# Pooled attention and a PReLU feed-forward network: the output tiles of chunks 1 to 8 stored by ACT's DMA queue

## The chip, the cores and the metric

The kernel runs on one core of a Trainium2 chip. The metric is the time of one execution on the device in microseconds; lower is better. The core has five engines that run side by side, each with its own list of instructions worked off in order: PE (matrix products), DVE and ACT (element-wise work), POOL (element-wise work) and SP, which here only begins DMA transfers. ACT can begin transfers too. A wait at the head of an engine's list holds everything behind it on that engine.

## The reference

Attention over 8 batches and 8 heads, with keys and values averaged over groups of 8 positions, and then a feed-forward network with a PReLU. Cut to its core:

```python
k_p = k.reshape(B, H, Sp, 8, D).mean(axis=3)      # 576 -> 72 positions; v_p alike
attn = softmax(q @ k_p.T / sqrt(D))
x = (attn @ v_p).transpose(0, 2, 1, 3).reshape(4608, 512)
h = x @ w_in                                      # 512 -> 2048
g = max(h, 0) + alpha * min(h, 0)
out = g @ w_out                                   # 2048 -> 512, float32
```

## The kernel before

The 4608 tokens go in 9 chunks of 512 tokens (chunk 0 to chunk 8). Every float32 operand is split into a high and a low float16 part, and each product is three matrix products. Chunk 0 has its own start phase (about the first 200 us, in which weights are loaded and converted as well). From chunk 2 on the first layer (FFN-1) is done in Strassen form: per chunk 4 blocks of 7 products, each product twelve matmuls at L964, with combined weights `wt` that SP loads from a DRAM buffer `ws` (L942, 896 KB each, eight per chunk). A result bank `m` of PSUM (two of them) is emptied by DVE (`join`, L977) or ACT (`keep`, L973) into buffers `c`; ACT scales them (L1115), DVE does the PReLU (L1119), ACT makes the high part `g` (L1123), POOL the low one (L1126). The second layer runs one block behind the first, on the rows of `g`: a step is six matmuls at L885 to L887 that add into one of four PSUM tiles of 128 tokens by 512. One product or one such step is called a piece below; PE alternates between them.

While PE works on a chunk, the attention of the next chunk is prepared beside it: loads of k, q and v by SP (L279), the maxima of q, k and v (ACT L407, a small PE product L233 on the tile `pd` that ACT writes at L230), scores (PE L667), softmax (DVE, ACT, POOL), four transposes `aT<-apad` that SP begins (L577), and the mix with v (PE L677).

After its last step an output tile is scaled into SBUF by ACT (`out_tile`, L875) and stored by `store` (L880), 256 KB. The SBUF tile comes from the pool `fp` with three buffers (the kind "f"), which also serves tiles of the attention (`ks`, `vs`); a buffer comes free when the store has landed. The four output tiles of a chunk thus need a buffer that an earlier store gives back.

The order on every engine is not the order of the code. All operations are recorded in a plan (`_Plan.add`: engine, assumed duration, what it comes after, a rank, and the kinds of buffers that it takes and gives). `_Plan.emit` then plays the plan through with the assumed durations and emits the operations in the order that this gives; an operation on "SP" counts as done `DMA_HOP` = 2.0 us after its end, on another engine 0.12 us (`HOP`). Since each choice depends on the times before it, another duration or engine for one operation reorders much of what comes later on all engines.

Of the kernel before, what the change touches and what calls it, by code (L numbers as in the profile page):

```python
# [21 lines left out]
SP = S // POOL  # L22
# [3 lines left out]
P = 128  # L26
# [60 lines left out]
class _Plan:  # L87
# [13 lines left out]
        self.fill = fill  # L101
        self.ops, self.room, self.port = [], {k: n * [0.0] for k, n in room.items()}, 0.0

    def add(self, engine, us, emit, *after, rank=0.0, take=None, give=None, two=False, ahead=0.0):
        kinds = lambda x: (x,) if isinstance(x, str) else tuple(x or ())
        op = dict(engine=engine, us=us, emit=emit, after=after, rank=rank, n=len(self.ops), take=kinds(take),
                  ahead=ahead, give=kinds(give), two=two or engine == "Pool")
        self.ops.append(op)
        return op

    def emit(self):
        ops, free = self.ops, {}
        mine = {id(op) for op in ops}
        follow, left, since, ready = [[] for _ in ops], [], len(ops) * [0.0], {}
        for op in ops:
            after = [d for d in op["after"] if id(d) in mine]
            for d in after:
                follow[d["n"]].append(op)
            left.append(len(after))
            if not after:  # L120
                ready.setdefault(op["engine"], {})[op["n"]] = op
        for _ in ops:
            picks = []
            for engine, some in ready.items():
                at = []
                for n, op in some.items():
                    t = max(free.get(engine, 0.0), since[n], self.port if op["two"] else 0.0)
                    need = {k: op["take"].count(k) for k in op["take"]}
                    if any(len(self.room[k]) < x for k, x in need.items()):
                        continue  # L130
                    t = max([t] + [sorted(self.room[k])[x - 1] for k, x in need.items()])
                    at.append((t, op["rank"], n))
                if at:
                    t0 = min(at)[0] + self.NEAR[engine]
                    picks.append(min((x for x in at if x[0] <= t0), key=lambda x: x[1:]))
            t, _, n = min(picks, key=lambda x: (x[0], x[2]))
            op = ops[n]
            engine = op["engine"]
            if engine == "PE" and self.fill:
                gap = t - free.get("PE", 0.0)  # L140
                if gap > self.IDLE:
                    self.fill(int((gap * 0.89 - (0.6 if free.get("PE") else 2.5)) / 0.109))
            free[engine] = t + op["us"]
            if op["two"]:
                self.port = t + op["us"]
            end = t + op["us"] + (self.DMA_HOP if engine == "SP" else self.HOP)
            for kind in op["take"]:
                self.room[kind].remove(min(self.room[kind]))
            for kind in op["give"]:
                self.room[kind].append(end)  # L150
            for x in follow[n]:
                since[x["n"]] = max(since[x["n"]], end + x["ahead"])
                left[x["n"]] -= 1
                if not left[x["n"]]:
                    ready.setdefault(x["engine"], {})[x["n"]] = x
            del ready[engine][n]
            op["emit"]()
# [3 lines left out]
def pooled_attention_prelu_ffn(ctx: ExitStack, tc: tile.TileContext, qT, kT, vT, kN, vN, w1, w2, alpha, out):  # L161
# [5 lines left out]
    nc = tc.nc  # L167
# [707 lines left out]
        nc.scalar.activation(o, ps, AF.Copy, scale=out_scale(c, i))  # L875
        return o

    def store(c, i, o):
        t0 = c * CH + i * P
        return nc.sync.dma_start(out=out[t0:t0 + P, :], in_=o)  # L880

    def ffn2_step(c, i, f, ps, first, final):
        ts_ = slice(i * P, i * P + P)
# [189 lines left out]
    def steady(plan, xd, td, used, loaded, made):  # L1073
        FFN, HIGH = 1e6, -1e6
# [74 lines left out]
        def out_items(c, b):  # L1149
            for k in range(2):  # L1150
                for i in range(TPC):
                    def item(k=k, i=i):
                        first, final = b == k == 0, b == NB - 1 and k == 1
                        fs = (4 * b + k, 4 * b + 2 + k)

                        def products():
                            if first:
                                acc[c, i] = ps_h.tile([P, DM], F32, tag="h", name="o")
                            for f in fs:
                                ffn2_step(c, i, f, acc[c, i], first and f == fs[0], final and f == fs[1])  # L1160
                        x = pe(1.3, products, *(g_at[c, b][f] for f in fs), take="h" if first else None,
                               give="g" if k == 1 and i == TPC - 1 else None)
                        if final:
                            o = []
                            y = plan.add("ACT", 0.69, lambda: o.append(out_tile(c, i, acc.pop((c, i)))), x, scaled["o", c],
                                         rank=HIGH, take="f", give="h")
                            plan.add("SP", 0.8, lambda: store(c, i, o[0]), y, rank=HIGH, give="f")
                    yield item

        for n in range(NB * (NC - 1) + 1):  # L1170
            c, b = 1 + n // NB, n % NB
# [61 lines left out]
```

## Time and profile before

| | us |
|---|---|
| median of 3 runs (lowest, highest) | 855.45 (854.04, 858.91) |
| the profiled execution | 858.35 |
| its span, from the first to the last instruction | 856.6 |
| PE busy | 807.3 |
| DVE busy | 591.7 |
| ACT busy | 478.7 |
| POOL busy | 426.0 |

The span is what the trace covers; the rest of the execution's time lies around it. PE's busy time counts matmuls as overlapping, so it is read here only for where PE is not busy. The clock that the throttle granted to PE and the DMA traffic are given by the profile as well.

### The profile page before, as it was taken

Reading aid. Unit: us, or ns where it says so; the run is one execution under the profiler, and the core shown is the slowest. Engines: PE = TensorE matmul, PEld = TensorE weight load, DVE = VectorE, ACT = ScalarE, POOL = GpSimd, SP = SyncE. Lnnn points to the kernel's source line nnn. Section 1 sums busy time; section 2 is a strip of 40 time slices with the busy share of each in tenths; the row PEclk is TensorE's granted clock in tenths of the full one; section 3 lists DMA queues with packets and bytes.
Section 4 is the critical chain, followed back from the end, with each engine's and each line's share of the span. In section 5 each row is a group of like instructions: output and inputs, shape, how many; then the busy total and the mean of one; then the engine's idle time right before and its main releaser. Section 6 shows DMA issues by size and latency. Waiting matters only on the chain.

```text
span 856.6 us, 15008 instructions
## 1 busy us (share of the span) xinstructions
PE 807.3 (94%) x5971; PEld 497.1 (58%) x5971; DVE 591.7 (69%) x880; ACT 478.7 (56%) x858; POOL 426.0 (50%) x433
## 2 busy tenths in 40 slices
PE   5679987899999889999999999999999999999998
PEld 4444453344456556665666666666666666666664
DVE  4969879897798776766986786677757544433442
ACT  6779996475455455655656564654655444223223
POOL 0255646767865466347546844653444434222222
PEclk9899999999999999999999999999999999999999
DMA  9678337229724891693298159525645534223201
GB/s 330 230 168 316 128 78 176 83 96 256 236 93 154 239 253 69 155 281 106 103 267 255 52 154 247 146 94 160 183 125 142 145 109 169 87 88 135 86 1 50
DMA packets 106198, 133.69 MB, mean 156 GB/s; under 512 B 78320, under 2 KB 80944, under 8 KB 106128
## 3 DMA queue, kind: packets, MB, share of 16 engines
q1 hardware_dynamic: 106128, 132.74, 51.5%
q8 instruction: 47, 0.77, 0.4%
q14 instruction: 23, 0.19, 0.1%
HBM read 96.48 MB, written 16.78 MB: 132 GB/s over the span
## 4 chain that ended last, share of the span: by engine, by line
PE 61%; DVE 9%; DMA 6%; ACT 4%; issue 2%; POOL 1%; SPq 0%; DVEq 0%; ACTq 0%; POOLq 0%
PE m L964 24%; PE o L885 10%; PE o L886 10%; PE o L887 10%; DMA qraw<-qT_dram 3%; DVE c L1119 2%; PE x L677 2%; PE s L667 1%; DVE c L977 1%; PE h L840 1%; PE h L842 1%; PE h L841 1%; ACT c L1115 1%; DMA aT<-apad 1%; DMA vraw<-vT_dram 1%
## 5 line engine op out<-in xcount | busy, mean ns | idle before, releaser
L964 PEld LDWEIGHTS <-wt 128*128 128x128 f16 x2352 | 228.3, 98 | 72.1 <-issue 3.3
L977 DVE TENSOR_TENSOR c<-m,c 128x512 f32<-128x512 f32 x196 | 134.6, 688 | 163.6 <-PE m L964 158.5
L1126 POOL TENSOR_TENSOR g<-c,g 128x512 f16<-128x512 f32 x112 | 136.4, 1229 | 205.4 <-ACT g L1123 130.6
L886 PE MATMUL o<-w,g 128*128 128x512 f16 x544 | 206.8, 380 | 4.6 <-DVE w L762 4.6
L885 PE MATMUL o<-w,g 128*128 128x512 f16 x544 | 207.3, 381 | 0.3 <-POOL g L1126 0.3
L887 PE MATMUL o<-w,g 128*128 128x512 f16 x544 | 206.8, 380 | 0.0
L964 PE MATMUL m<-x,wt 128*128 128x256 f16 x1344 | 166.1, 273 | 4.2 <-DVE c L977 2.3
L1115 ACT ACTIVATE c<-c,rp 128x512 f32<-128x512 f32 x112 | 75.5, 714 | 118.9 <-DVE c L977 114.6
L1119 DVE SCALAR_TENSOR_TENSOR c<-c,al 128x512 f32<-128x512 f32 x112 | 102.7, 939 | 31.0 <-ACT c L1115 30.5
L964 PE MATMUL m<-xt,wt 128*128 128x256 f16 x1008 | 123.8, 273 | 0.0
L887 PEld LDWEIGHTS <-g 128*128 128x128 f16 x576 | 56.6, 98 | 73.7 <-issue 6.6
L885 PEld LDWEIGHTS <-g 128*128 128x128 f16 x576 | 56.5, 98 | 52.5 <-issue 4.3
L1123 ACT CAST g<-c 128x512 f16<-128x512 f32 x112 | 67.9, 617 | 32.0 <-DVE c L1119 31.0
L886 PEld LDWEIGHTS <-g 128*128 128x128 f16 x576 | 56.6, 98 | 46.2 <-issue 1.1
L489 POOL TENSOR_TENSOR vraw<-vraw 72x512 f32<-72x512 f32 (+1 forms) x56 | 63.4, 1145 | 30.7 <-DMA vraw<-vT_dram 17.7
L569 POOL TENSOR_TENSOR apad<-e,apad 128x448 f16<-128x448 f32 x36 | 38.4, 1067 | 59.5 <-ACT apad L566 58.8
L566 ACT CAST apad<-e 128x576 f16<-128x576 f32 x72 | 46.1, 669 | 23.0 <-POOL e L561 11.0
L859 POOL TENSOR_TENSOR g<-t,g 128x512 f16<-128x512 f32 x32 | 39.3, 1240 | 35.7 <-ACT g L856 28.1
L627 POOL TENSOR_TENSOR xf<-xf 128x256 f32<-128x256 f32 x48 | 38.0, 791 | 35.1 <-ACT xf L622 32.3
L841 PE MATMUL h<-x,w 128*128 128x512 f16 x128 | 48.5, 379 | 1.5 <-DVE x L604 1.5
L840 PE MATMUL h<-x,w 128*128 128x512 f16 x128 | 48.6, 380 | 0.0
L842 PE MATMUL h<-x,w 128*128 128x512 f16 x128 | 48.5, 379 | 0.0
(156 smaller groups left out, 1081.1 us busy)
## 6 DMA issues: line engine op xcount, KB each, us to landing
wt<-ws SPq DMA_DIRECT2D x56, 896.0 KB
w<-w_dram SPq DMA_DIRECT2D x16, 1024.0 KB
out_dram<-o SPq DMA_DIRECT2D x36, 256.0 KB
qraw<-qT_dram SPq DMA_DIRECT2D x17, 512.0 KB
vraw<-vT_dram SPq DMA_DIRECT2D x28, 288.0 KB
kraw<-kT_dram SPq DMA_DIRECT2D x12, 576.0 KB
ws<-o SPq DMA_DIRECT2D x8, 512.0 KB
ws<-w SPq DMA_DIRECT2D x8, 256.0 KB
```

The costliest lines, as they stand in the source:

```text
L489: nc.gpsimd.tensor_tensor(out=o, in0=y, in1=z, op=ALU.add)
L840: nc.tensor.matmul(ps, w[:, 1, ks_], x[:, 0], start=(n == 0), stop=False)
L841: nc.tensor.matmul(ps, w[:, 0, ks_], x[:, 1], start=False, stop=False)
L885: nc.tensor.matmul(ps, g[:, 1, ts_], w[:, 0], start=first, stop=False)
L886: nc.tensor.matmul(ps, g[:, 0, ts_], w[:, 1], start=False, stop=False)
L887: nc.tensor.matmul(ps, g[:, 0, ts_], w[:, 0], start=False, stop=final)
L964: nc.tensor.matmul(ps[:, p], w[:, lw], x[:, lx], start=(j == n == 0), stop=(j == 1 and n == 2))
L977: nc.vector.tensor_tensor(out=self.part(b, o), in0=self.t[b, m], in1=self.part(b, i), op=ALU.add)
L1115: nc.scalar.activation(u, u, AF.Copy, scale=rp[:, f:f + 1])
L1119: nc.vector.scalar_tensor_tensor(out=u, in0=u, scalar=al[:, f:f + 1], in1=u, op0=ALU.mult, op1=ALU.max)
L1123: nc.scalar.copy(out=g_tile(c, f)[:, 0], in_=st.row(b, i, p)[0])
L1126: nc.gpsimd.tensor_tensor(out=g_tile(c, f)[:, 1], in0=st.row(b, i, p)[0], in1=g_tile(c, f)[:, 0], op=ALU.subtract)
```

## The change

Each of the 32 output tiles of chunks 1 to 8 is stored by a transfer that ACT begins (`nc.scalar`), directly from ACT's list; the four of chunk 0 stay on SP. In the plan the store is an operation of ACT of 0.1 us where it was one of SP of 0.8 us; the flag `far` keeps its 2.0 us until it counts as done.

```diff
--- before.py
+++ after.py
@@ -101,10 +101,10 @@
         self.fill = fill
         self.ops, self.room, self.port = [], {k: n * [0.0] for k, n in room.items()}, 0.0
 
-    def add(self, engine, us, emit, *after, rank=0.0, take=None, give=None, two=False, ahead=0.0):
+    def add(self, engine, us, emit, *after, rank=0.0, take=None, give=None, two=False, ahead=0.0, far=False):
         kinds = lambda x: (x,) if isinstance(x, str) else tuple(x or ())
         op = dict(engine=engine, us=us, emit=emit, after=after, rank=rank, n=len(self.ops), take=kinds(take),
-                  ahead=ahead, give=kinds(give), two=two or engine == "Pool")
+                  ahead=ahead, give=kinds(give), far=far or engine == "SP", two=two or engine == "Pool")
         self.ops.append(op)
         return op
 
@@ -143,7 +143,7 @@
             free[engine] = t + op["us"]
             if op["two"]:
                 self.port = t + op["us"]
-            end = t + op["us"] + (self.DMA_HOP if engine == "SP" else self.HOP)
+            end = t + op["us"] + (self.DMA_HOP if op["far"] else self.HOP)
             for kind in op["take"]:
                 self.room[kind].remove(min(self.room[kind]))
             for kind in op["give"]:
@@ -875,9 +875,9 @@
         nc.scalar.activation(o, ps, AF.Copy, scale=out_scale(c, i))
         return o
 
-    def store(c, i, o):
+    def store(c, i, o, by=nc.sync):
         t0 = c * CH + i * P
-        return nc.sync.dma_start(out=out[t0:t0 + P, :], in_=o)
+        return by.dma_start(out=out[t0:t0 + P, :], in_=o)
 
     def ffn2_step(c, i, f, ps, first, final):
         ts_ = slice(i * P, i * P + P)
@@ -1164,7 +1164,7 @@
                             o = []
                             y = plan.add("ACT", 0.69, lambda: o.append(out_tile(c, i, acc.pop((c, i)))), x, scaled["o", c],
                                          rank=HIGH, take="f", give="h")
-                            plan.add("SP", 0.8, lambda: store(c, i, o[0]), y, rank=HIGH, give="f")
+                            plan.add("ACT", 0.1, lambda: store(c, i, o[0], nc.scalar), y, rank=HIGH, give="f", far=True)
                     yield item
 
         for n in range(NB * (NC - 1) + 1):
```

Up to the stores of chunk 1 all engines have the same rows in the same order; behind them the plan's order differs on all of them. On SP, at the stores of chunk 1 (`wt<-ws_125` and so on are the loads of combined weights, `ws_130<-w` and `ws_128<-o` writes of such weights to DRAM):

```order
 L922 DMA ws_128<-o_2611 128x2048
 L942 DMA wt<-ws_125 128x3584
-L880 DMA out_dram<-o 128x512 x2
-L942 DMA wt<-ws_126 128x3584
-L880 DMA out_dram<-o 128x512 x2
+L942 DMA wt<-ws_126 128x3584
 L942 DMA wt<-ws_127 128x3584
 L904 DMA ws_130<-w_275 128x1024
 L905 DMA ws_130<-w_275 128x2x256
```

The two loads of weights that stood behind two and four stores now follow the load of `ws_125` directly.

On ACT, at the same place (`o` is the output tile, `c` the buffers of FFN-1, `g` the high part): before,

```order
L875 ACTIVATE o<-o,os 128x512
L1115 ACTIVATE c<-c,rp 128x512 x2
L875 ACTIVATE o<-o,os 128x512
L1123 CAST g<-c 128x512 x2
L875 ACTIVATE o<-o,os 128x512
L1115 ACTIVATE c<-c,rp 128x512
L875 ACTIVATE o<-o,os 128x512
L1115 ACTIVATE c<-c,rp 128x512
```

and now

```order
L875 ACTIVATE o<-o,os 128x512
L880 DMA out_dram<-o 128x512
L1115 ACTIVATE c<-c,rp 128x512 x2
L875 ACTIVATE o<-o,os 128x512
L880 DMA out_dram<-o 128x512
L1123 CAST g<-c 128x512 x2
L875 ACTIVATE o<-o,os 128x512
L880 DMA out_dram<-o 128x512
L1115 ACTIVATE c<-c,rp 128x512
L875 ACTIVATE o<-o,os 128x512
L880 DMA out_dram<-o 128x512
L1115 ACTIVATE c<-c,rp 128x512
```

Each store follows the activation that writes its tile and waits for it; the scaling and casts of FFN-1 stand behind it. Most of these stores also wait, by the program, for one transfer of SP that was begun earlier and shares the store's semaphore.

On SP, at the stores of chunk 2, in the time in which the attention of chunk 4 is transposed and the k, q and v of chunk 5 are loaded: before,

```order
L577 DMA_TRANSPOSE aT<-apad_95 128x16x128
L279 DMA kraw<-kT_dram 128x1152
L880 DMA out_dram<-o 128x512
L577 DMA_TRANSPOSE aT<-apad_96 128x16x128
L880 DMA out_dram<-o 128x512
L942 DMA wt<-ws_127 128x3584
L880 DMA out_dram<-o 128x512
L942 DMA wt<-ws_128 128x3584
L880 DMA out_dram<-o 128x512
L279 DMA kraw<-kT_dram 128x1152
L279 DMA qraw<-qT_dram 128x1024
```

and now

```order
L577 DMA_TRANSPOSE aT<-apad_95 128x16x128
L279 DMA kraw<-kT_dram 128x1152
L577 DMA_TRANSPOSE aT<-apad_96 128x16x128
L279 DMA kraw<-kT_dram 128x1152
L942 DMA wt<-ws_127 128x3584
L577 DMA_TRANSPOSE aT<-apad_95 128x16x128
L942 DMA wt<-ws_128 128x3584
L279 DMA qraw<-qT_dram 128x1024
```

The four stores are gone from between the loads, and the third transpose stands ahead of the load of q, where it stood behind it.

On PE the pieces keep their order, and only the attention's products move between them. The mix of chunk 3 stands 3 pieces earlier than before, that of chunk 4 stands 7 pieces earlier, those of chunks 5 and 6 stand 8 and 4 pieces later, and those of chunks 7 and 8 stand where they were. The three small products L233 on the maxima of chunk 5 (k and q) stood ahead of the mix of chunk 4 and now stand behind it, 7 pieces later than before; those of chunk 7 stand one piece later. On SP, two transposes and two loads of weights stood between the loads of k for chunk 7 and that of its q; now none does.

## Rows read from the trace of the kernel before

**Rows 1.** The page: the span, and the busy time of each engine.

```profile
span 856.6 us, 15008 instructions
PE 807.3 (94%) x5971; PEld 497.1 (58%) x5971; DVE 591.7 (69%) x880; ACT 478.7 (56%) x858; POOL 426.0 (50%) x433
```

**Rows 2.** Busy time by stretches of 50 us from 250 us on: stretch, its length, busy us (instructions) of PE, PE's weight loads, DVE, ACT and POOL, the granted clock, the DMA share and GB/s.

```profile
250.00:300.00 50.00, 46.16 (x394) 30.12 (x393) 42.04 (x60) 26.20 (x54) 29.22 (x29) 1.00 0.58 170
300.00:350.00 50.00, 46.44 (x362) 29.93 (x360) 34.84 (x55) 28.13 (x56) 29.52 (x34) 0.97 0.55 159
350.00:400.00 50.00, 48.01 (x386) 31.81 (x385) 32.27 (x55) 26.06 (x43) 26.39 (x27) 1.00 0.79 207
400.00:450.00 50.00, 50.00 (x440) 32.47 (x437) 43.48 (x65) 30.34 (x59) 27.97 (x29) 1.00 0.52 163
450.00:500.00 50.00, 48.61 (x391) 32.43 (x389) 34.63 (x51) 29.28 (x58) 34.31 (x35) 1.00 0.50 156
500.00:550.00 50.00, 47.80 (x374) 31.16 (x372) 34.86 (x55) 26.56 (x44) 25.39 (x24) 1.00 0.78 207
550.00:600.00 50.00, 50.00 (x448) 32.71 (x447) 38.38 (x58) 28.65 (x57) 27.45 (x30) 1.00 0.35 111
```

**Rows 3.** What PE waited for between 250 and 600 us: total us, times, longest.

```profile
PE pm L233 <- ACT pd L230: 3.6, 2, 2.0
PE x L677 <- DMA aT<-apad: 2.9, 1, 2.9
PE m L964 <- DVE c L977: 2.3, 2, 2.0
PE m L964 <- DMA wt<-ws: 1.5, 2, 1.3
PE s L667 <- ACT e L546: 1.3, 2, 0.7
PE x L677 <- ACT xf L622: 0.7, 1, 0.7
```

**Rows 4.** What SP's queue waited for at the line of the stores, in the whole run: total us, times, longest.

```profile
SPq L880 <- ACT o L875: 160.5, 32, 48.4
```

**Rows 5.** SP's instructions in order of time around the stores of chunk 1 and up to the last transpose of chunk 3: start, us (two or more in a row are merged with their waits), line.

```profile
264.94 2.94 SPq L880 DMA_DIRECT2D out_dram<-o  x2
267.93 0.42 SPq L942 DMA_DIRECT2D wt<-ws  x1
270.14 1.63 SPq L880 DMA_DIRECT2D out_dram<-o  x2
271.86 0.39 SPq L942 DMA_DIRECT2D wt<-ws  x1
...
276.09 0.32 SPq L922 DMA_DIRECT2D ws<-o  x1
...
310.63 5.93 SPq L577 DMA_TRANSPOSE aT<-apad  x1
```

**Rows 6.** PE and DVE in order of time in the same stretch: start, us, instruction; in brackets the idle time before it and what ended it.

```profile
272.63 0.83 PE L964 MATMUL m<-x,wt 128*128 128x256 f16 x6 [1.35 <-DMA wt<-ws]
283.20 1.48 PE L964 MATMUL m<-x,wt 128*128 128x256 f16 x12 [2.03 <-DVE c L977]
...
285.82 1.47 PE L964 MATMUL m<-x,wt 128*128 128x256 f16 x12
...
282.45 0.69 DVE L977 TENSOR_TENSOR c<-m,c 128x512 f32<-128x512 f32 x1 [2.53 <-DMA ws<-o]
```

**Rows 7.** PE in order of time at the mix of chunk 3.

```profile
318.61 0.91 PE L677 MATMUL x<-aT,v 88*64 88x320 f16 x12 [2.95 <-DMA aT<-apad]
319.45 2.13 PE L964 MATMUL m<-x,wt 128*128 128x256 f16 x12
```

**Rows 8.** SP's instructions in order of time around the stores of chunk 2.

```profile
358.64 3.35 SPq L577 DMA_TRANSPOSE aT<-apad  x1
362.09 0.52 SPq L880 DMA_DIRECT2D out_dram<-o  x1
...
369.09 0.33 SPq L880 DMA_DIRECT2D out_dram<-o  x1
...
370.25 0.39 SPq L279 DMA_DIRECT2D qraw<-qT_dram  x1
...
385.65 5.06 SPq L577 DMA_TRANSPOSE aT<-apad  x1
```

**Rows 9.** PE in order of time: the small products on the maxima and the mix of chunk 4, and the small product on the maxima of chunk 7.

```profile
390.11 0.22 PE L233 MATMUL pm<-pd,ones 128*128 128x128 bf16 x1 [1.99 <-ACT pd L230]
...
395.52 1.08 PE L677 MATMUL x<-aT,v 88*64 88x256 f16 x16
...
542.31 0.22 PE L233 MATMUL pm<-pd,ones 128*128 128x128 bf16 x1 [1.56 <-ACT pd L230]
```

**Rows 10.** ACT in order of time: the fourth output tile of chunk 2, and what it waited for.

```profile
368.37 0.69 ACT L875 ACTIVATE o<-o,os 128x512 f32<-128x512 f32 x1 [1.25 <-DMA out_dram<-o]
```

**Rows 11.** The views of two lines, the stores and the transposes: how many, the shortest, median and longest time in ns that SP was held by one, first and last start, forms.

```profile
L880 SPq DMA_DIRECT2D out_dram<-o x36: 332/338/530, 172.3 to 853.6; - x36
...
L577 SPq DMA_TRANSPOSE aT<-apad x36: 1694/2652/5930, 40.6 to 683.5; - x36
```

**Rows 12.** The chain that ended last, its last piece: start, us, engine, tile and line.

```profile
852.90 0.69 ACT o L875
```

## The prediction

> **What bounds the kernel now.** I read the page first: PE is busy in 807.3 of 856.6 us, no other engine above 591.7 [rows 1]. So I looked for the places where PE is not busy, by stretches. The change can act only from the first store of chunk 1 on, at 264.94 us [rows 5], since all engines have the same list up to there. From 250 to 600 us PE is busy for 337.0 of 350 us: the seven stretches leave 3.84, 3.56, 1.99, 0, 1.39, 2.20 and 0 us, together 12.98 us [rows 2]. The rows to see there are the full ones: where PE shows 50.00 of 50 it sets the pace alone, and no better list for SP can win anything. So nearly all that can be won is 13 us of waits, plus what a slow clock costs after one of them. The third view tells what these waits were for [rows 3]: small products on maxima that ACT brings late (3.6 us), the mix of chunk 3, which waits for a transpose (2.9), banks of FFN-1 that DVE empties late (2.3), loads of combined weights (1.5), and smaller ones behind ACT.
>
> Are the stores behind these? In the whole run SP's list stands at them for 160.5 us until ACT has the tile ready [rows 4]. That alone costs nothing; what matters is which load stands behind one and is waited for.
>
> **The change part by part.** The sum is made on the profiled execution, 858.35 us. The median of the runs, 855.45, is 2.9 us lower, and I take these 2.9 off at the end.
>
> A. Stores of chunk 1. SP was at the stores from 264.94 to 267.88, and only then began the load of the weights that PE waited 1.35 us for at 272.63; the next load came after two more stores, at 271.86 [rows 5, 6]. In the new list both follow the earlier load directly and wait only for PE to release their buffers, by the order some pieces before the end of the first output tile. They can start some 3 to 6 us earlier, and the wait of 1.35 us goes. The second wait has a longer path: DVE finishes a tile of combined weights, SP writes it out from 276.09, and the buffer comes free only when it has landed, which held DVE's join until 282.45 and PE until 283.20 [rows 5, 6]. The write took 6.3 us, with the late loads ahead of it. With those out of the way I expect about the 4.7 us that the load begun at 267.93 took to PE's start at 272.63, or less. But ACT now begins four stores before its cast of that tile, at 0.34 us each [rows 11], and DVE gets it a little later. Between 3.38 us (both waits gone) and 0 I take 2.5 won: the first wait shifts PE, but the second is set by DVE, so the two do not add up.
>
> B. Mix of chunk 3. PE waited 2.95 us for the fourth transpose, and the product behind it then took 2.13 us where the same twelve matmuls took 1.48 [rows 6, 7]; the granted clock of this stretch of 50 us was 0.97, that is 1.5 us lost [rows 2]. So up to 4.5 us hang on this wait. In the new list the loads of v ahead of that transpose no longer stand behind a write of weights, so it comes earlier than 310.63 [rows 5]. But PE meets the mix 3 pieces earlier, and with A's 2.5 us that is about 6.4 us (a piece takes 1.3 us: a product begun at 283.20 and the next at 285.82 have a step between them [rows 6]). What the transpose wins is needed in full. I put nothing down here; the ends are 4.5 won and 2 lost.
>
> C. Stores of chunk 2. The first store is followed by a transpose that holds SP for 3.35 us, so that the second store leaves only at 362.09; the fourth tile on ACT waits 1.25 us for a buffer; its store leaves at 369.09; and the load of q for chunk 5 behind it at 370.25 [rows 8, 10]. Its maxima reach PE late: 1.99 us of wait at 390.11 [rows 9]. Without stores between them these loads can leave earlier, and the small products moved 7 pieces back. The wait should go. But the load of q now stands behind the third transpose, which waits for POOL and ACT, and the mix of chunk 4 comes first. Between 1.99 and 0 I take the middle, 1.0.
>
> D. Maxima of chunk 7: 1.56 us of wait at 542.31 [rows 9]. The load of their q no longer stands behind two transposes. Middle again: 0.8.
>
> E. Cost on ACT. The trace shows no store begun by ACT. On SP one holds the list for 0.332 to 0.530 us, median 0.338 [rows 11]: 32 of them are 10.8 us on ACT, which is busy for 478.7 of 856.6 [rows 1], so most of it falls into gaps. 16 of them (chunks 1 to 4) lie in the stretch with waits, 5.4 us. PE waits for ACT at five places there (rows of `pd`, `e` and `xf`) [rows 3]. If half of these have a store shortly ahead, that is 0.8 us; the ends are 0 and 5.4. From 550 us on PE is full [rows 2] and the cost is hidden behind it as long as ACT has its gaps.
>
> F. The end. The last output tile is scaled at 852.90 for 0.69 us, and the span ends 3.0 us later, with its store [rows 1, 12]. ACT needs 0.69 plus 0.34 us for a tile, less than the 1.3 us in which PE delivers one, so nothing queues there: 0.
>
> Sum: 858.35 - 2.5 - 1.0 - 0.8 + 0.8 = 854.85; less 2.9 gives **852.0 us**.
>
> **The rivals.** 1. The waits go for good: A 3.4, B 4.5 (without the wait the clock stays up), C 2.0, D 1.6, against 0.8 on ACT, 10.7 us in all; I take 9, since a new order hardly leaves none: 846.5 us. For it: every one of these waits has a load behind a store or a transpose in its history. Against it: the mix of chunk 3 comes up earlier too.
>
> 2. No change, 855.5 us. PE is full in two of seven stretches [rows 2], and what is won early is given back at the next product of the attention, which the plan has moved forward in proportion. SP has time: what is truly saved is 32 times 0.338 us of its list [rows 11], on which PE does not wait. The Trainium skill (DMA: Bandwidth & Descriptors, Issuing engines are not separate DMA queues) says as much of transfers begun on several engines: they run on the same DMA engines, and only the time of beginning one is saved. The rows speak against that being all, since SP's list stood 160.5 us at these stores [rows 4].
>
> 3. Slower: the mix of chunk 4 comes before its inputs. PE meets it 7 pieces earlier, 9.1 us. Before, its fourth transpose left SP at 385.65 and the mix ran at 395.52 without a wait [rows 8, 9]. If that transpose leaves no earlier, PE is 9.1 us behind at this point, less C's 2.0: 855.45 + 7.1 = 862.5 us. It decides when the transpose leaves less than about 5 us earlier. For it: the load of q and the transposes share SP, and ACT now has stores between its casts. Against it: SP lost 362.09 to 369.09 to stores there [rows 8].
>
> 4. ACT is held while SP begins a transpose. SP is held for 1.7 to 5.9 us by one, 36 times 2.65 us or 11% of the span [rows 11]. If a store on ACT had to wait for that, 3 to 4 of 32 would be hit, more in chunks 1 to 4, by 1.3 to 5.9 us each; with half of it on PE's path some 6 us: 858 to 861 us. No row bears on it. The Trainium skill (Perfetto Trace Analysis, DMA Instruction — HWDGE (DVE, Sync)) lets a sequencer wait for a descriptor generator that two sequencers share, which would be this mechanism; no run so far shows it.
>
> **How the numbers follow.** Forecast 0.40, rival 1 0.27, rival 2 0.12, rival 3 0.14, rival 4 0.07. 0.5% of the time, about what a measurement of this kernel can tell from no change, is 4.3 us: faster is below 851.2, slower above 859.7. Faster: rival 1 and an eighth of the forecast, 0.32. Slower: rival 3, most of rival 4: 0.20. The rest is 0.48. The range leaves out the lower edge of rival 1 and most of rival 3: 845.5 to 861 us.
>
> **What would show it.** Right: no wait of PE for `wt` near 270 us, the join near 282 us released 2 us earlier, the load of q for chunk 5 not behind a store, and less than 10 us of idle PE from 250 to 600. Wrong: PE idle for 4 us or more at the mix of chunk 3 or 4 (rival 3), a store on ACT that holds it for over 1 us while SP is at a transpose (rival 4), or new waits behind ACT between 600 and 850, where PE was full.

## The result, and the profile after

The kernel after takes 866.27 us (863.32 to 867.37) where the kernel before took 855.25 us on the same chip: a ratio of 1.0109, 95% interval 1.0081 to 1.0137. It is slower by 11 us, where 3 were to be won, and lies outside the range. Its profiled execution took 865.44 us, so that run and the profiled one of before are 7.1 us apart; the rest is the scatter of single runs. One of the seven runs of old_order_no_hold below took 1404 us; its ratio leaves that run out, and without it the median is 852.20.

The page and the seven stretches of 50 us, against [rows 1] and [rows 2]; q10 is the new queue, ACT's own, with 32 stores:

```profile
span 863.7 us, 15011 instructions
PE 813.2 (94%) x5971; PEld 499.0 (58%) x5971; DVE 589.2 (68%) x880; ACT 478.7 (55%) x858; POOL 423.4 (49%) x433
...
q10 hardware_dynamic: 4608, 8.39, 2.6%
```

```profile
250.00:300.00 50.00, 44.05 (x378) 28.67 (x377) 41.58 (x60) 25.90 (x53) 28.70 (x29) 1.00 0.55 161
300.00:350.00 50.00, 49.75 (x413) 32.42 (x412) 42.43 (x63) 29.70 (x57) 34.32 (x36) 1.00 0.51 169
350.00:400.00 50.00, 44.25 (x326) 28.45 (x324) 27.24 (x43) 24.93 (x41) 27.17 (x27) 0.97 0.76 207
400.00:450.00 50.00, 49.45 (x441) 32.75 (x439) 35.99 (x63) 25.55 (x50) 17.95 (x21) 1.00 0.37 125
450.00:500.00 50.00, 49.43 (x370) 32.20 (x369) 38.45 (x49) 29.24 (x48) 34.81 (x35) 1.00 0.68 193
500.00:550.00 50.00, 46.34 (x367) 30.06 (x366) 33.11 (x57) 28.39 (x58) 22.40 (x25) 0.97 0.64 195
550.00:600.00 50.00, 49.31 (x455) 32.45 (x454) 36.94 (x54) 27.71 (x54) 29.64 (x33) 1.00 0.35 105
```

PE now leaves 17.4 us of these 350, where it left 13.0, and two stretches instead of one have a granted clock of 0.97, which is 1.5 us more lost (0.03 of 50). To see where the loss ends, take ACT at the first output tile of chunk 1 and that of chunk 5, in the kernel before:

```profile
264.23 0.69 ACT L875 ACTIVATE o<-o,os 128x512 f32<-128x512 f32 x1 [2.21 <-PE o L887]
...
614.33 0.69 ACT L875 ACTIVATE o<-o,os 128x512 f32<-128x512 f32 x1 [0.70 <-PE o L887]
```

and in the kernel after:

```profile
265.30 0.69 ACT L875 ACTIVATE o<-o,os 128x512 f32<-128x512 f32 x1 [2.21 <-PE o L887]
...
621.40 0.69 ACT L875 ACTIVATE o<-o,os 128x512 f32<-128x512 f32 x1 [0.91 <-PE o L887]
```

This stretch took 350.1 us and now 356.1. From there to the first output tile of chunk 8 both take 234.6 to 234.7 us, and ahead of the stretch both have the same lists. So 6.0 of the 7.1 us lie in chunks 1 to 4, and the 4.4 us of idle PE and the 1.5 of clock make up 5.9 of them. I use this stretch as a measure below. It is taken from one execution of each run: old_order_act_chunks_5_to_8, which leaves the stores of chunks 1 to 4 as they were, gave 347.1, so 3 us of it can be scatter.

What PE waits for there, against [rows 3]:

```profile
PE m L964 <- ACT c L973: 6.6, 4, 2.9
PE m L964 <- DMA wt<-ws: 4.4, 2, 2.8
PE o L885 <- ACT o L875: 3.0, 1, 3.0
...
PE s L667 <- ACT e L546: 0.7, 1, 0.7
PE x L677 <- DMA aT<-apad: 0.6, 1, 0.6
```

The waits of [rows 3] that the change was to remove are mostly gone: 3.6 us for `pd`, 2.0 of the 2.3 for DVE's join and most of the 2.9 for the transpose; the one for weights grew from 1.5 to 4.4. In their place stand 9.6 us on ACT that were not there, its copy of a product (`c`, L973) and its output tile (`o`, L875). ACT is no busier than it was: 478.7 us in both pages. It stands still. What ACT waited for at L875 from 250 us on, before and then after (total us, times, longest):

```profile
ACT o L875 <- DMA out_dram<-o: 2.6, 3, 1.3
```

```profile
ACT o L875 <- DMA out_dram<-o: 21.8, 5, 5.7
```

The output tile needs one of three buffers, and one comes free only when an earlier store has landed. ACT in order of time at chunk 2, in the kernel after:

```profile
358.94 0.68 ACT L875 ACTIVATE o<-o,os 128x512 f32<-128x512 f32 x1
359.65 0.34 ACTq L880 DMA_DIRECT2D out_dram<-o  x1
...
367.33 0.69 ACT L875 ACTIVATE o<-o,os 128x512 f32<-128x512 f32 x1 [5.43 <-DMA out_dram<-o]
368.04 0.35 ACTq L880 DMA_DIRECT2D out_dram<-o  x1
368.44 0.72 ACT L1115 ACTIVATE c<-c,rp 128x512 f32<-128x512 f32 x1 [0.43 <-ACT o L875]
369.07 0.56 ACT L973 COPY c<-m 128x512 f32<-128x512 f32 x1
...
375.99 0.69 ACT L875 ACTIVATE o<-o,os 128x512 f32<-128x512 f32 x1 [5.74 <-DMA out_dram<-o]
```

ACT's list goes in order: behind the tile that stands at 367.33 is the copy at 369.07, and PE waits for both. PE at the same place, and at chunk 4:

```profile
369.68 1.47 PE L964 MATMUL m<-x,wt 128*128 128x256 f16 x12 [1.86 <-ACT c L973]
...
376.73 0.59 PE L885 MATMUL o<-w,g 128*128 128x512 f16 x1 [2.97 <-ACT o L875]
...
547.39 2.72 PE L964 MATMUL m<-x,wt 128*128 128x256 f16 x12 [2.87 <-ACT c L973]
```

The last row shows the second price: after 2.87 us of standing still, twelve matmuls took 2.72 us, where 1.47 is usual. The granted clock of this stretch (547.39 to 550.11 us) is 0.50, the lower of its two levels (1.2 and 2.4 GHz).

The begin itself is not late: each of the 32 stores begins 0.03 us after its tile is done, so the semaphores that the stores share with SP's transfers held none of them. Why the buffer comes back late is in the chain that ended last. Two pieces of it at chunk 2 before, and at the same chunk after (start, us from the store's begin to its landing):

```profile
362.09 2.61 DMA out_dram<-o
...
365.51 2.77 DMA out_dram<-o
```

```profile
359.65 7.59 DMA out_dram<-o
...
368.04 7.92 DMA out_dram<-o
```

The tile at 367.33 starts 0.09 us after the first of these has landed (359.65 and 7.59 are 367.24), the one at 375.99 0.03 us after the second. SP's list around these two stores, in the kernel after:

```profile
359.40 0.33 SPq L942 DMA_DIRECT2D wt<-ws  x1
362.30 4.51 SPq L577 DMA_TRANSPOSE aT<-apad  x1
366.90 0.53 SPq L942 DMA_DIRECT2D wt<-ws  x1
367.52 0.38 SPq L279 DMA_DIRECT2D qraw<-qT_dram  x1
367.96 0.91 SPq L279 DMA_DIRECT2D vraw<-vT_dram  x2
```

Each store has loads of SP begun just ahead of it (896 KB at 359.40 and at 366.90), and a transpose or more loads behind. In SP's own list the store went first and the loads stood behind it, as [rows 8] show. The records of single packets in the trace give the parts. Of the 32 stores, 11 met no packet of SP on the way to their first: their first packet ran 0.84 to 0.88 us after the begin. For the other 21 it was 1.28 to 4.98 us. Three of these stores, three of the run with stores of 8 KB (below), and one of each kind without SP:

```
store (256 KB)  begun   first packet  last packet ended
chunk 1         268.62  after 3.22    after 5.49 us
chunk 2         359.65        4.14          6.91
chunk 2         368.04        4.11          7.43
chunk 5         622.12        0.84          1.68
store (8 KB)
chunk 2         358.55  after 1.98    after 6.19 us
chunk 2         366.11        3.83          6.59
chunk 4         532.74        4.38          8.56
chunk 8         854.78        0.84          1.05
```

### The profile page after: what moved, and what is told of

Same layout as the page of the kernel before. It is cut to its first block, busy times and chain, and to the rows that moved or that the text cites. A ratio compares the mean times of both kernels' runs of the same rounds, so it can differ in the third digit from the quotient of the medians.

```text
span 863.7 us, 15011 instructions
## 1 busy us (share of the span) xinstructions
PE 813.2 (94%) x5971; PEld 499.0 (58%) x5971; DVE 589.2 (68%) x880; ACT 478.7 (55%) x858; POOL 423.4 (49%) x433
## 4 chain that ended last, share of the span: by engine, by line
PE 59%; DVE 7%; DMA 6%; ACT 5%; POOL 4%; issue 2%; SPq 1%; ACTq 0%; DVEq 0%; POOLq 0%
PE m L964 23%; PE o L885 10%; PE o L887 10%; PE o L886 10%; DMA out_dram<-o 4%; PE x L677 1%; DMA qraw<-qT_dram 1%; PE s L667 1%; PE h L840 1%; PE h L841 1%; PE h L842 1%; POOL g L1126 1%; SPq L577 1%; ACT o L875 1%; POOL vraw L489 1%
## 5 line engine op out<-in xcount | busy, mean ns | idle before, releaser
L1119 DVE SCALAR_TENSOR_TENSOR c<-c,al 128x512 f32<-128x512 f32 x112 | 96.5, 881 | 49.9 <-ACT c L1115 49.6
L841 PE MATMUL h<-x,w 128*128 128x512 f16 x128 | 49.2, 384 | 1.5 <-DVE x L604 1.5
L840 PE MATMUL h<-x,w 128*128 128x512 f16 x128 | 49.3, 385 | 0.0
L842 PE MATMUL h<-x,w 128*128 128x512 f16 x128 | 49.0, 383 | 0.0
```

Source lines behind the costliest of these rows:

```text
L840: nc.tensor.matmul(ps, w[:, 1, ks_], x[:, 0], start=(n == 0), stop=False)
L841: nc.tensor.matmul(ps, w[:, 0, ks_], x[:, 1], start=False, stop=False)
L1119: nc.vector.scalar_tensor_tensor(out=u, in0=u, scalar=al[:, f:f + 1], in1=u, op0=ALU.mult, op1=ALU.max)
```

## The experiments

All times are medians; "before" is the kernel before on the same chip. The last two columns come from each run's profiled execution: ACT's waits at the output tile for landed stores from 250 us on, and the stretch from the first output tile of chunk 1 to that of chunk 5.

| run | us | before | ratio (95%) | ACT waits, us | stretch, us |
|---|---|---|---|---|---|
| the kernel after | 866.27 | 855.25 | 1.0109 (1.0081 to 1.0137) | 21.8 | 356.1 |
| new_order_sp | 869.33 | 856.95 | 1.0143 (1.0114 to 1.0172) | 12.0 | 359.3 |
| old_order_act | 861.83 | 856.95 | 1.0065 (1.0040 to 1.0090) | 13.5 | 352.8 |
| new_order_16_columns | 862.77 | 856.95 | 1.0057 (1.0027 to 1.0087) | 19.8 | 354.0 |
| old_order_16_columns | 853.92 | 856.95 | 0.9947 (0.9925 to 0.9968) | 2.3 | 344.7 |
| new_order_no_hold | 852.03 | 856.22 | 0.9942 (0.9912 to 0.9972) | 1.9 | 341.9 |
| old_order_no_hold | 852.54 | 856.22 | 0.9948 (0.9923 to 0.9973) | 1.9 | 343.2 |
| old_order_extra_starts | 856.74 | 856.22 | 0.9995 (0.9968 to 1.0021) | 4.1 | 347.9 |
| new_plan_late_landing | 863.59 | 856.22 | 1.0076 (1.0042 to 1.0110) | 5.6 | 357.0 |
| old_order_act_chunks_1_to_4 | 859.51 | 856.51 | 1.0030 (1.0001 to 1.0058) | 16.5 | 350.9 |
| old_order_act_chunks_5_to_8 | 856.82 | 856.51 | 0.9997 (0.9966 to 1.0029) | 1.2 | 347.1 |
| new_order_four_buffers | 886.25 | 856.51 | 1.0325 (1.0292 to 1.0357) | 0 | 337.0 |
| old_order_four_buffers | 886.04 | 856.51 | 1.0324 (1.0281 to 1.0367) | 0 | 337.8 |
| new_order_buffer_of_their_own | 873.54 | 857.71 | 1.0167 (1.0124 to 1.0210) | 22.6 | 347.4 |
| old_order_buffer_of_their_own | 864.30 | 857.71 | 1.0082 (1.0057 to 1.0107) | 2.9 | 336.4 |
| new_order_own_buffer_later | 877.39 | 857.27 | 1.0224 (1.0182 to 1.0266) | 18.0 | 363.9 |
| old_order_own_buffer_later | 861.42 | 857.27 | 1.0042 (1.0012 to 1.0072) | 2.4 | 352.2 |
| new_order_pause_only | 851.12 | 855.81 | 0.9939 (0.9913 to 0.9966) | 0 | 341.3 |
| new_order_hold_only | 865.43 | 855.81 | 1.0102 (1.0066 to 1.0138) | 27.7 | 355.8 |

**Queue and order apart.** The new order with the stores begun by SP:

```diff
-plan.add("ACT", 0.1, lambda: store(c, i, o[0], nc.scalar), y, rank=HIGH, give="f", far=True)
+plan.add("ACT", 0.1, lambda: store(c, i, o[0]), y, rank=HIGH, give="f", far=True)
```

> The changed kernel's plan and its order on PE, DVE, ACT and POOL, but SP begins the stores again, at the places where the plan emits them. Theory 1 (stores on a queue of their own no longer go ahead of SP's loads, land late, and ACT stands at the next output tile for a buffer): stores land in about 3 us again, ACT waits under 6 us for them in all, 853 to 859 us. Rival 2 (the new order of the plan is itself worse, whoever begins the stores): 863 to 868 us. Rival 3 (the 0.34 us that each store takes of ACT's list, with the pause behind it): 853 to 859 us.

And the old order with the stores begun by ACT at the same places:

```diff
-return nc.sync.dma_start(out=out[t0:t0 + P, :], in_=o)
+return (nc.scalar if c else nc.sync).dma_start(out=out[t0:t0 + P, :], in_=o)
```

> The plan and order of the kernel before, word for word on PE, DVE and POOL; only the transfer of each output tile of chunks 1 to 8 is begun by ACT, directly from its list, not by SP. Theory 1: SP's loads start beside the stores, the stores land in 4 to 8 us, ACT waits some 15 us for buffers, 862 to 868 us. Rival 2: 853 to 858 us, since the order is the old one. Rival 3: 860 to 868 us, but with little wait of ACT for stores.

The first, 869.33 us, missed my theory and fell a little beyond the rival's range. In this list, made for other stores, a transpose came 6.4 us late, and maxima 5.5 (what PE waited for in that run from 250 us on):

```profile
PE pm L233 <- ACT pd L230: 7.5, 2, 5.5
PE x L677 <- DMA aT<-apad: 6.4, 1, 6.4
```

The second, 861.83 us, just under my range, costs 4.9 us in the old order. Not all of that is the queue: at these places, chosen for SP, some stores stand in ACT's list behind the next output tile, which itself had to wait, so that a store of chunk 1 began 3.56 us and one of chunk 4 4.95 us after its tile was done. So neither order nor queue is innocent by these two; the waits for landed stores are there in both.

**The store's size.** Stores of chunks 1 to 8 of 16 columns, 8 KB instead of 256:

```diff
-return by.dma_start(out=out[t0:t0 + P, :], in_=o)
+return by.dma_start(out=out[t0:t0 + P, :16 if c else DM], in_=o[:, :16 if c else DM])
```

> The changed kernel with every instruction in place, but each store of chunks 1 to 8 writes only 16 of the 512 columns (8 KB, not 256 KB); the other columns of these rows are left out. The 32 transfers are still begun by ACT. Theory 1: they land in 2 to 3 us, ACT waits under 4 us for buffers, 852 to 858 us. Rival 2: 862 to 867 us. Rival 3: 862 to 867 us, as the number of stores on ACT is the same.

> The kernel before with stores of 16 of 512 columns for chunks 1 to 8 (the rest of these rows is left out), still begun by SP. A control for what the bytes of the stores cost by themselves. Theory 1: only the 2.6 us of ACT's wait for buffers can go, 852 to 855 us. Rivals 2 and 3: 854 to 856 us. If the bytes were dear by themselves (8.4 of 133.7 MB), both kernels with small stores would win the same.

I had not expected the waits to stay: 19.8 us of ACT with a 32nd of the bytes, and a time in the range of both rivals. Of the stores of 8 KB, too, 21 met packets of SP before their first. Their last packet ended 1.92 to 8.56 us after the begin, median 3.62; of those of 256 KB it was 3.04 to 7.43, median 5.41. Without SP's packets it is 1.05 and 1.67. So most of the time is not the store's own transfer; it comes where SP's transfers are under way. By the sign that I had set, the bytes are dear by themselves as well: both kernels won some 0.5% (1.0109 to 1.0057, and 1 to 0.9947). The loss between the two, 1.1%, stays as it was.

**The hold taken away.** The same 16 columns, but from a constant tile: queue, begin and bytes as in the last pair, and no output tile's buffer waits for the landing.

```diff
-return by.dma_start(out=out[t0:t0 + P, :], in_=o)
+return by.dma_start(out=out[t0:t0 + P, :16 if c else DM], in_=pool[:, :16] if c else o)
```

> The changed kernel with all instructions in place, each store of chunks 1 to 8 begun by ACT at its place, but it writes 16 columns from a constant tile, so that no transfer holds the output tile's buffer (the results of these chunks are not written). Against the run with 16 columns from the output tile (862.8 us, ACT waiting 19.8 us for buffers) only the hold is gone, and the pause of some 0.4 us in which the store waits for its activation. Theory 1, now narrowed to the hold (a store begun on its own queue lands late behind SP's backlog whatever its size, and ACT stands at the next output tile for a buffer): 853 to 857 us. Rival 2 (the new order is worse by itself): 860 to 864 us. Rival 3 (ACT's time for beginning 32 stores): 860 to 864 us.

> The order of the kernel before, stores of chunks 1 to 8 begun by ACT, 16 columns from a constant tile, so that no buffer is held (these results are not written). Against the old order with ACT's full stores (861.8 us) and the old order with SP's 16 columns (853.9 us). Theory 1 (the hold): 852 to 855 us. Rival 2 says nothing of it. Rival 3 (ACT's time): 858 to 862 us.

862.77 falls to 852.03 us, and both orders are now alike. For stores that hold no buffer, the new order is thus no worse than the old. Of the 1.7% between the kernel after (1.0109) and this run (0.9942), 0.5% went with the bytes, and the 10.7 us from 862.77 with the hold and with one thing more that is taken apart below.

**The begin by itself.** The kernel before, with 32 more transfers of 8 KB begun by ACT, from a constant to scratch memory:

```diff
+c and nc.scalar.dma_start(out=dram.tile([P, 16], F32, name=f"x{c}_{i}"), in_=pool[:, :16])
```

> The kernel before with its stores on SP, and in addition 32 transfers of 8 KB that ACT begins at the places where the stores are emitted, from a constant tile to scratch memory: ACT's time for beginning a transfer, without a hold of a buffer that ACT needs. Theory 1: 854 to 857 us. Rival 3: 859 to 864 us. The extra transfers take semaphores of the ring of eight too, so that some waits of SP move.

856.74 beside 856.22 us: no price that can be measured. These begins wait for no tile, and ACT made them while it worked on one; a begin that stands behind its tile is tested below (the pause).

**A plan that knows.** The kernel after, with a plan told that a store on ACT takes 0.75 us and its buffer returns 6 us later:

```diff
-end = t + op["us"] + (self.DMA_HOP if op["far"] else self.HOP)
+end = t + op["us"] + (6.0 if op["far"] and engine == "ACT" else self.DMA_HOP if op["far"] else self.HOP)
...
-plan.add("ACT", 0.1, lambda: store(c, i, o[0], nc.scalar), y, rank=HIGH, give="f", far=True)
+plan.add("ACT", 0.75, lambda: store(c, i, o[0], nc.scalar), y, rank=HIGH, give="f", far=True)
```

> The changed kernel, with the plan told what the traces showed: a store begun by ACT holds ACT for 0.75 us (0.34 us and the pause behind it) and its buffer comes back 6.0 us after it, not 0.1 and 2.0. The plan reorders all engines by it, so ACT should do other work while a buffer is out. Theory 1: ACT's wait for buffers falls from 21.8 us to under 8, 853 to 861 us. Rival 2 (a new order of this plan is worse than the old one, whatever it assumes): 862 to 870 us.

A miss: ACT's waits fell to 5.6 us, but the time only to 863.59, which is in the rival's range. PE now waits 5.0 us for weights and 3.2 for an output tile; that the plan puts the tiles later, with three buffers and a late landing, is my reading and not tested. The 0.75 us were too much, since the pause of 0.41 us has the 0.34 of the begin in it.

**Where it counts.** The edit of old_order_act for half of the chunks, once each:

```diff
-return nc.sync.dma_start(out=out[t0:t0 + P, :], in_=o)
+return (nc.scalar if 0 < c < 5 else nc.sync).dma_start(out=out[t0:t0 + P, :], in_=o)
...
+return (nc.scalar if c > 4 else nc.sync).dma_start(out=out[t0:t0 + P, :], in_=o)
```

> The order of before, with only the 16 stores of chunks 1 to 4 begun by ACT. Theory 1 (ACT stands at the next output tile for a buffer that a late landing holds, and PE waits where it has nothing else to do, which is only before 600 us): nearly the whole loss of the run with 32 such stores (861.8 us), so 860 to 863 us, with 10 us or more of waits of ACT for landed stores. Rival (each store begun by ACT costs its share, wherever it stands): half of the loss, 858 to 859 us.

> The order of before, with only the 16 stores of chunks 5 to 8 begun by ACT. Theory 1: PE has had its last wait by then, so 855 to 857 us, the time of the kernel before, though stores land late there too. Rival (each costs its share): 858 to 859 us.

Chunks 5 to 8 cost nothing that can be measured, as expected. Chunks 1 to 4 cost 3.0 us: 859.51 us lies between the rival's range and mine. The intervals of this run and of all 32 (1.0030 and 1.0065) overlap.

**More buffers, every output written.** A fourth buffer for a third of the exponentials:

```diff
-ROOM = dict(d=3, W=8, L=4, f=3, e=3, v=3, qp=2, vp=2, aT=1, S=2, h=4, m=0, g=0, x=0, X=0)
+ROOM = dict(d=3, W=8, L=4, f=4, e=2, v=3, qp=2, vp=2, aT=1, S=2, h=4, m=0, g=0, x=0, X=0)
```

> The kernel after with 4 instead of 3 buffers for output tiles, paid for with one buffer of the exponentials (2 instead of 3); the plan knows both numbers, so the whole order is made anew. Read against the next run, which is the kernel before with the same numbers. Theory 1: with a fourth buffer ACT stands for landed stores under 6 us (21.8 us in the kernel after), and the time is within 4 us of the next run's. Rival (something else than the buffer makes the stores on ACT dear): it is 8 to 13 us above the next run, as after is above before.

> The kernel before with 4 instead of 3 buffers for output tiles and 2 instead of 3 for the exponentials, in a plan made for these numbers; the control of the run above. Both theories: 853 to 866 us, since the priorities in the plan were chosen for the old numbers. If it is under 853 us, the third buffer had been short in the kernel before too.

The two agree within 0.2 us, no wait of ACT for a landed store is left, and the stretch, 337.0 and 337.8 us, is among the shortest. But the whole list is another one, and 41 us are lost ahead of it. The control itself missed its range by 20 us. So I tried to give up that buffer later, and to give the further one to the odd output tiles:

```diff
-o = fp.tile([P, DM], F32, tag="f", name="o")
+o = (op if c and i % 2 else fp).tile([P, DM], F32, tag="f", name="o")
...
-                                         rank=HIGH, take="f", give="h")
+                                         rank=HIGH, take="fF"[i % 2], give="h")
```

> The kernel after, with a further buffer from the start of the steady phase on (chunk 1 and later): it takes the place of one of the three buffers of the exponentials, which is given up at that point only, so the time ahead stays as it was. The odd output tiles of chunks 1 to 8 use this buffer alone, the even ones the three shared ones as before; the plan knows it. Read against the next run. Theory 1: ACT stands for landed stores under 8 us in all, where it stood 21.8 us, and the stretch from the first output tile of chunk 1 to that of chunk 5, 356.1 us in the kernel after, falls to 340 to 348 us; the time is 848 to 857 us and within 5 us of the next run's. Rival (a store begun on ACT is dear for another reason, and the two runs with four buffers agreed because their order was another one altogether): 862 us or more, and 8 us or more above the next run.

> The kernel before with the same further buffer from the steady phase on for the odd output tiles, stores begun by SP. Theory 1: 848 to 855 us, since the kernel before has 2.6 us of such waits itself and lost little more with smaller stores held (853.9) than with none held (852.5). Rival: the same as the kernel before, 855 to 858 us, or more, if the attention misses its third buffer of exponentials in the steady phase too.

The first output tile came at 280 us instead of 265 in both: in the new list the attention of chunk 2 has only two buffers of exponentials. With the third given up only behind this attention:

```diff
+if c == 1:
+    plan.add("SP", 0.0, grow, *[op for op in plan.ops if "e" in op["give"]], rank=-1e9, take="e", give="F")
```

> As the kernel after with a buffer of its own for the odd output tiles, but the buffer of the exponentials is given up only when the attention of chunk 2 is through, so that the order is that of the kernel after until the stores of chunk 1. Theory 1 (the landing of the stores holds buffers): the stretch from the first output tile of chunk 1 to that of chunk 5 is 341 to 350 us (347.4 in the run before this, 356.1 in the kernel after), with the first store at 264 to 267 us again, so 851 to 860 us; ACT still stands 10 to 25 us for landed stores, since one buffer for all odd tiles makes the fourth tile wait for the store of the second. Rival (the further buffer helped only because the order of chunk 1 had changed): 356 us in that stretch and 864 us or more.

> As the kernel before with the same further buffer, given up only when the attention of chunk 2 is through. Theory 1: the stretch from chunk 1 to chunk 5 is 335 to 343 us (336.4 in the run before this, 350.1 in the kernel before), the first store at 263 to 266 us, so 841 to 849 us: faster than both kernels, and 5 to 12 us below the run above, since SP's stores land in their turn and let the buffers go sooner. Rival: 850 us or more, as the kernel before with no store held (852.5).

Both pairs missed their ranges, and stood 9 and 16 us apart. By my own bound that speaks for the rival; but ACT still stood 22.6 and 18.0 us for landed stores in the new order, against 2.9 and 2.4 in the old. So these runs did not take the hold away, since one buffer for all odd tiles makes each wait for the one before it; that they lose elsewhere through the missing buffer is argued, not shown. As a remedy they failed; as a test of the cause they leave it open.

**Hold and pause apart.** The run without a hold had lost something else too: ACT's pause of 0.41 us between the end of an output tile and its next work (the 0.43 in the rows of ACT above), 13 us in all. The store has to wait for the tile and is begun in this pause, which takes 0.34 of it; without a hold ACT began the store while it worked on the tile. The pause alone, with a store of 4 columns from a small tile of its own (to make room, the buffers of another small tile, `nb`, went from 4 to 2):

```diff
+if c:
+    o = tiny.tile([P, 4], F32, tag="tiny", name="tiny")
+    nc.scalar.activation(o, ps[:, :4], AF.Copy, scale=out_scale(c, i))
```

> As the kernel after, but each store of chunks 1 to 8 takes 4 columns from a small tile of its own (four buffers), which ACT writes behind the output tile by one more short instruction; the results of these chunks are not written. ACT still has to wait for the end of its own instruction before it begins the store, the pause of 0.41 us that the run without a hold did not have, but no buffer of an output tile is held. Theory 1 (the held buffer): 851 to 856 us, near the run without a hold (852.0), with under 4 us of waits of ACT for landed stores. Rival (it is the pause of ACT after each of 32 tiles, 13 us in all): 860 us or more.

The hold alone, with every output written: ACT begins a store one instruction later, when the tile is done (in the code that emits the plan).

```diff
+if engine == "ACT" and op["far"]:
+    late = op["emit"]
+    continue
 op["emit"]()
+if engine == "ACT" and late:
+    late, run = None, late
+    run()
```

> As the kernel after, with every output written, but ACT begins each store one instruction of its list later, so that the output tile is finished by then and ACT need not pause for it; the buffers are held as in the kernel after, or some 0.7 us longer. Theory 1: no better than the kernel after, 863 to 870 us, with 18 us or more of waits of ACT for landed stores. Rival (the pause): 852 to 858 us, though these waits stay.

Both came out as the theory of the held buffer said: 851.12 us with the pause, 865.43 with the hold. What ACT waited for at its output tile in the latter, from 250 us on:

```profile
ACT o L882 <- DMA out_dram<-o: 27.7, 7, 6.9
```

Otherwise the lists of these two are those of the kernel after, but for the short instruction of the first; in the second, one store of chunk 3 began as late as 3.64 us after its tile. They differ in the bytes of the stores too, so the clean pair is at small stores: 862.77 us (a ratio of 1.0057) with hold and pause and 19.8 us of waits, 851.12 (0.9939) with the pause alone and none. The hold is the price, and the pause and the begin in it are not.

## Why the prediction was wrong

**The step that failed is E**, the cost on ACT. It priced a store on ACT by the time for which it holds the list, 0.338 us, and took its ends, 0 and 5.4 us, from that alone. That price was right (the view of the stores' line after, in ns: shortest, median, longest)

```profile
L880 ACTq DMA_DIRECT2D out_dram<-o x32: 338/338/382, 266.0 to 860.6; - x32
```

and, by old_order_extra_starts and new_order_pause_only, worth nothing that can be measured. What no step priced is when the store lands, who holds a buffer until then, and what stands behind the next taker in ACT's list. PE's waits on ACT grew from 5.6 us of other kinds [rows 3] to 9.6 of this kind. The sign was on record: C read the 1.25 us in [rows 10] only as a delay of the load of q behind that store, not as a buffer that comes back just in time. "Without stores between them these loads can leave earlier", it says. They could; and what they passed is the store, which now lands later.

**A** failed as well. The first load of weights left at 268.49 us, where it was 267.93 [rows 5]; counted from the first output tile that is 3.19 us, where it was 3.70, so it won 0.5 us and not 3 to 6. SP's wait at the two loads was for PE to release the buffer:

```profile
SPq L942 <- PE m L964: 22.7, 2, 22.4
```

So the stores in front of the first load had cost half a us. The second left some 4 us earlier, and no wait of PE went by it: the wait for weights became 1.56 us from 1.35, and one of 2.81 us came at 299.15. DVE's join did come earlier: PE's wait for it fell from 2.3 to 0.3 us in all.

**B** came out at its good end. The mix of chunk 3 ran without a wait, and the clock of its stretch stayed at 1.00:

```profile
314.69 1.08 PE L677 MATMUL x<-aT,v 88*64 88x192 f16 x16
```

That is 2.9 us of wait and 1.5 of clock won, where I put 0. **C and D**: the waits for maxima (1.99 and 1.56 us) are gone, more than the 1.0 and 0.8 I took. **F** holds: the last output tile starts at 859.93 and the span ends 3.1 us after it is done.

Without the hold, and with smaller stores, the change comes out at 851.1 to 852.0 us in two runs, beside a forecast of 852.0. That is luck: small stores alone won 3.0 us in the old order (old_order_16_columns), and the old order without the hold took 852.54. What is left to the new list, whose waits A to D were to pay, is under 1 us and within the noise.

**Rivals.** 1 had half the story: most waits of [rows 3] went, but others came. 2 fell with the time, though the runs without a hold fit its doubt that waits won on PE would show in the time. The Trainium skill (DMA: Bandwidth & Descriptors, Issuing engines are not separate DMA queues) has transfers of several engines interleave on the same DMA engines, with only the time of beginning saved. The runs agree: in the old order, stores of 8 KB took 853.92 us begun by SP and 852.54 begun by ACT without a hold, 0.5% under before in both. What the move added here is 1.28 to 4.98 us to the first packet where SP's packets were under way, and 0.84 to 0.88 where none were. 3 did not occur: PE waited 0.59 us at the mix of chunk 4. 4 did not occur: three stores were begun while SP was held by a transpose, of 2.7 to 4.9 us, and each held ACT for 338 or 339 ns. The lock that the Trainium skill describes (Perfetto Trace Analysis, DMA Instruction — HWDGE (DVE, Sync)) is not to be seen in these 32. Only this rival had the slower side come from ACT, and it was wrong that it would come from the begin. Of the signs named for being wrong none showed: the new waits behind ACT came before 600 us, and PE has no wait from 600 to 870. Two signs of being right failed: PE still waited for weights (1.56 us before 273.92), and it was idle for 17.4 us from 250 to 600, not under 10.

**Still open.** Whether a store waits for SP's packets in the DMA engines or ahead of them, where its descriptors are made, no view here tells. That SP's packets are what a store waits for is read from where they meet; no run has the stores of chunks 1 to 4 held without SP's transfers beside them. Why the new order with SP's stores is slower still (869.33 us) is argued from its two late inputs, not shown. ACT's waits for landed stores do not give the time by themselves: 5.6 us of them go with 863.59 us, 16.5 with 859.51. And no version with every output written beat the kernel before.

## What to carry to other kernels

When a transfer moves to another engine's queue, do not price its begin; price its landing. Ask which buffer stays held until then, which instruction takes that buffer next, and what stands behind it on an engine that goes in order. A small row such as "ACT <- DMA out" of 1.3 us says that the buffers are just enough, and that a landing a few us later can cost time wherever another engine has no slack.

In the list of one queue the order is yours: a store ahead of a load goes first. On a second queue it is not. A move that frees the loads can make the store land behind them.

## What the runs showed of the hardware

A store of 8 KB on ACT's queue took up to 8.56 us to its last packet while SP's loads and transposes were under way, and 1.05 us when none were; one of 256 KB took 1.67 us in that case. A pause of 0.41 us of ACT behind the tile, in which it begins the store, 32 times, cost nothing measurable (851.12 beside 852.03 us). And stores of 8 KB instead of 256 KB, begun by SP in the old order, won 3 us, although PE waits for none of them.
